# Block-sparse attention into a swish layer: the planner's order replaced by a written one, with new opening casts and paired score steps

## The chip, the cores and the metric

The kernel runs on one core of a Trainium2 chip. Its time is that of one execution in microseconds of device time; before the change three executions took 300.73, 301.71 and 305.26, median 301.71.

## The reference

Attention over four batches of eight heads, 768 positions of 64, in blocks of 32 positions. A query block sees its own block and its two neighbours, the first and the last block, and three blocks drawn per query block (`sampled_blocks`); the first and the last query block see everything. Its output, all heads of a position side by side, goes through a layer of 2048 hidden columns.

```python
scores = scale * np.matmul(q, k.transpose(0, 1, 3, 2))
...
scores = np.where(mask, scores, -1000000000.0)
scores = scores - np.max(scores, axis=-1, keepdims=True)
attn = np.exp(scores)
attn = attn / (np.sum(attn, axis=-1, keepdims=True) + 1e-09)
return np.matmul(attn, v).astype(np.float32)
...
h = x @ w_in
g = h * (1.0 / (1.0 + np.exp(-beta * h)))
return (g @ w_out).astype(np.float32)
```

## The kernel before

**Attention by pairs.** The 22 inner query blocks of a batch are handled in pairs, 44 pairs in all, numbered `n` from 0 to 43. Per pair the program makes these tasks, named by kind and number:

- `kg`: POOL copies six drawn key blocks into the tile `KG` (line 710; the block numbers are loaded to registers first, line 704); `kn`: the neighbour blocks, on POOL or DVE. There are three `KG` buffers.
- `vg`: DMAs on the SP queue that gather value blocks from a table `VT` in memory into `VG` (line 810); for the first four pairs TensorE picks the drawn blocks with one-hot matmuls (`pick`, line 825; `pickv` copies them out).
- `sc`: scores, a first set of matmuls that writes the mask (line 849) and a second that adds the products (line 862), in 64x32 tiles of the array, into two PSUM banks. From pair 33 on, two pairs share one step and take four banks (`TWO = 33`).
- `mx`: maxima on DVE (line 884); `ex`: exponentials on ACT with their sums (line 892), two per bank; `rc` or `hl`: reciprocals on DVE; `nrm`: normalisation of the probabilities `PP`, on POOL (line 915); for pairs below 11 it is folded into the output product (line 953) instead.
- `tp`: transpose on TensorE (line 929) or, from pair 31, by DMA (`tpd`); `ptv`: its copy to `PT` on DVE or ACT (line 330 or 328); `av`: the product with the values (lines 963 and 971); `rs`, `xv`: copies of the result into `xT`, the input of the layer.

The first and last query block of each batch go through `gs`, `gm`, `ge`, `gr`, `gn`, `gt`, `gptv`, `gav`, `gx` (lines 1026 to 1100) with whole rows of 768 scores. K and Q of a batch are loaded, for batch 0 cast on DVE (line 538), transposed on TensorE in half-width tiles (`trK`, `trQ`, line 632) and copied out (`evK`, `evQ`); V is rearranged and written to the table (`vperm`, `permV`, `vtab`).

**The layer.** It works in eight groups `G` of 256 or 512 positions. `h` makes one chunk of 128 hidden columns (line 1155), `tanh` on ACT (line 1161) and `stt` on DVE (line 1166) its activation `g`, `y` a quarter of an output tile (line 1182, four matmuls of 512 columns), `oe` its copy and `od` its DMA. A group's first chunk needs `xT` of the pairs it covers. Weights come by POOL's DMA queue in bulk loads: `win` (line 557, quarters of the hidden columns, two row chunks each), `wout` (line 563), and then K, Q and V of the next batch (line 588). A one-element copy (`touch`, line 543) holds each set back until the value gathers of pair 2 have landed.

**What sets the order.** Every task has an engine or a choice of two, a planned duration, dependencies, a priority, and PSUM banks that it opens or closes. `Plan.run` simulates the engines with these numbers and issues, at each moment, the ready task of the best priority; an `OFFSET` table shifts priorities. Each engine then executes its tasks in the order that comes out, and the bank numbers are those that the plan handed out. Waits between engines are semaphores that follow from the data.

Of the kernel before, what the change touches and what calls it, by code (L numbers as in the profile page):

```python
# [20 lines left out]
BIAS = {("nrm", "DVE"): 2.0, ("gn", "DVE"): 1.5}  # L21


class Task:
    def __init__(self, name, eng, dur, emit, deps=(), prio=0.0, lat=0.0,
                 opens=(), closes=(), moe=False, dma=0.0, slack=0.0, hw=0, bulk=None):
        self.on = {eng: dur} if isinstance(eng, str) else dict(eng)
        self.name, self.eng, self.dur, self.emit = name, None, None, emit
        self.deps = [d for d in deps if d is not None]
# [4 lines left out]
        self.tiling = Plan.TILING.get(self.kind, 0)  # L34
# [3 lines left out]
class Plan:  # L38


    HOP = 0.18
# [3 lines left out]
    MARGIN, DMARGIN = 1.0, 1.0  # L45


    TILING = {"sc": 1, "gs": 1, "av": 2, "gav": 2, "trK": 2, "trQ": 2}
    CHANGE, KEEP = 0.1, 0.0
    YOUNG = {"PE": 0, "DVE": 0, "ACT": 0.0, "POOL": 0.5, "SP": 0.0}  # L50
    YIELD = 20

    OFFSET = {'gt': 5, 'gav': 10, 'trK': 7.6, 'oe': 2.2, 'vg': -0.6, 'vv': -14.0, 'pick': -1.2, 'av0': 0.8, 'ptv0': -3.8, 'xv0': 3.7, 'vg0': 0.9, 'sc1': -2.5, 'kg1': 12.5, 'kn1': -11.1, 'mx1': -15, 'vg1': -5, 'av2': -5, 'kg2': 2.8, 'kn2': 4.2, 'hl2': 5.2, 'rs2': -5, 'kg3': -11.2, 'ex3': 0.3, 'rs3': -0.6, 'kg4': -15, 'rs4': 7.8, 'kn5': 18.1, 'ptv5': 6.3, 'rs5': 39.6, 'av6': -0.3, 'kg6': 2.5, 'kn6': -60, 'ptv6': -2.4, 'mx6': 4.5, 'sc7': 15.7, 'tp7': 21.7, 'av7': 1.3, 'rs7': 1.6, 'sc8': 0.4, 'hl8': -3.7, 'xv8': -17.7, 'av9': -14.9, 'kg9': -6.0, 'kn9': 15, 'mx9': -15, 'ex9': -0.6, 'hl9': 19.8, 'rs9': 15, 'sc10': 21.3, 'tp10': 0.8, 'av10': 15, 'kg10': 2.9, 'kn10': -15, 'mx10': 30, 'vg10': 30, 'sc11': -60, 'av11': 15, 'ex11': 5, 'xv11': -1.7, 'av12': 0.5, 'kn12': -2.5, 'ptv12': 1.2, 'rs12': -0.3, 'xv12': 26.5, 'tp13': -0.2, 'kn13': 4.0, 'rs13': -3.7, 'xv13': -41.1, 'av14': 15, 'kg14': -15, 'kn14': -30, 'rs14': 24.8, 'xv14': 6.6, 'ptv15': 30, 'xv15': -24.7, 'mx0.0': 0.7, 'mx0.1': -9.9, 'mx1.1': -3.1, 'ex1.1': 5.7, 'ex2.0': -2.1, 'ex4.1': -15, 'mx7.1': 56.3, 'gn1': -22.5, 'vperm0.0': -0.6, 'trQ1': 11.7, 'trQ2': 11.1, 'trK3': 2.2, 'trQ3': -0.4, 'castQ': 2.6, 'tabK2': -34.6, 'tabK3': 8.6, 'ttQ2': 19.9, 'ldV3': 0.9, 'pick1': 9.2, 'pickv': 30, 'ldV0.1': 0.1, 'evK0': -6.3, 'evQ0': -1.2, 'tanh0': 5.1, 'stt1': -14.2, 'h3': 0.5, 'y3': -1.4, 'oe3': -8.0, 'y4': 1.4, 'tanh4': 9.0, 'oe4': 1.7, 'h5': 15.9, 'y5': -1.2, 'stt5': 3.2, 'h6': -60, 'y6': 11.9, 'tanh7': 60, 'stt7': -19.4}

    def __init__(self, n_banks, moe_banks):
        self.tasks = []
        self.n_banks, self.moe_banks = n_banks, moe_banks
        self.bank = {}
# [6 lines left out]
    def run(self):  # L65
        tasks = self.tasks
        attention_left = sum(1 for t in tasks if t.opens and not t.moe)
        succ = {}
        need = {}
        for t in tasks:  # L70
            need[t] = len(t.deps)
            for d in t.deps:
                succ.setdefault(d, []).append(t)
        readers = {}
        for t in tasks:
            for b in t.closes:
                readers[b] = readers.get(b, 0) + 1
        ready_at = {t: 0.0 for t in tasks}
        engines = sorted({e for t in tasks for e in t.on})
        free = {e: 0.0 for e in engines}  # L80
        waiting = {e: [] for e in engines}
        ring_at = hw_at = 1.0
        lanes = [0.0] * 8
        issued = 0

        tiling = 0
# [14 lines left out]
        def release(t):  # L101
            for e in t.on:
                waiting[e].append(t)
# [1154 lines left out]
```

## Time and profile before

| | us |
|---|---|
| time, median of three runs (lowest, highest) | 301.71 (300.73, 305.26) |
| span of the profiled execution | 302.9 |
| POOL busy, share of the span | 170.0, 56% |

The profile is that of another execution than the three timed ones, and no time of its own is given beside its span; the span stands between the median and the highest of them. Lines of the trace name the engine, the line of the code, the operation, the tile written and the tiles read. An `x8` behind a row says that eight instructions are merged in it. A time in brackets is the engine's idle time before the row, and what ended it. PE is TensorE's matmuls, PEld its weight loads. In a view of stretches the number after each engine's busy time is its count of instructions, and the last three columns are the granted clock (1.00 is full), the share of time in which the DMA engines were busy, and GB/s.

### The profile page before, as it was taken

How to read it: one execution, taken by the hardware profiler on the slowest of the kernel's cores; microseconds unless marked ns; L12 is line 12 of the kernel's file. 1: busy time of each engine (PE TensorE's matmuls, PEld its weight loads, DVE VectorE, ACT ScalarE, POOL GpSimd, SP SyncE). 2: the span in 40 equal slices, each digit the busy share in tenths (PEclk: the TensorE clock that was granted, in tenths of full speed). 3: DMA queues.
4: the chain of work that ended last, by engine and by line, in shares of the span. 5: the costliest groups of instructions: out<-in, count | busy, mean ns of one | idle time of the engine just before them, and what ended most of it. 6: DMA issues, size and time to landing. Idle time of an engine off the chain costs nothing.

```text
span 302.9 us, 11451 instructions
## 1 busy us (share of the span) xinstructions
PE 279.5 (92%) x4109; PEld 173.8 (57%) x4109; DVE 237.5 (78%) x556; ACT 218.6 (72%) x641; POOL 170.0 (56%) x513
## 2 busy tenths in 40 slices
PE   2599879999998799999999999999999999999993
PEld 1465668758846576665556555545554544555671
DVE  5848987999899998999999739999888834762150
ACT  3357657888789598799889749896787768763360
POOL 5057995034579957899777538677976654000000
PEclk9999957999999999999999999999999999999999
DMA  7999999979978852299933643248465446541102
GB/s 248 365 294 171 205 232 231 228 142 265 213 126 167 181 192 72 84 173 162 237 99 106 202 154 106 67 110 167 120 158 119 126 106 181 137 121 53 53 36 69
DMA packets 57170, 47.55 MB, mean 157 GB/s; under 512 B 19733, under 2 KB 53142, under 8 KB 57114
## 3 DMA queue, kind: packets, MB, share of 16 engines
q1 hardware_dynamic: 44736, 35.48, 41.3%
q0 software_dynamic: 12320, 11.27, 24.7%
q8 instruction: 32, 0.52, 0.7%
q14 instruction: 24, 0.20, 0.2%
q10 hardware_dynamic: 58, 0.07, 0.1%
HBM read 45.23 MB, written 9.44 MB: 180 GB/s over the span
## 4 chain that ended last, share of the span: by engine, by line
PE 49%; DVE 23%; issue 7%; ACT 6%; POOL 6%; DMA 5%; POOLq 2%; SPq 0%; DVEq 0%; ACTq 0%
PE bank L1155 17%; PE bank L1182 14%; DVE ST L884 5%; PE bank L825 4%; DVE g L1166 4%; PE bank L929 3%; POOL KG L710 3%; DMA g<-in_k_dram 3%; DVE SG L1040 3%; POOL PP L915 2%; PE bank L963 2%; PE bank L971 2%; ACT PP L892 2%; PE bank L632 2%; ACT t L1161 2%
## 5 line engine op out<-in xcount | busy, mean ns | idle before, releaser
L1155 PE MATMUL bank<-xT,w_in_sb 128*128 128x256 f16 (+1 forms) x512 | 93.8, 330 | 1.5 <-DVE g L1166 1.5
L892 ACT ACTIVATE PP<-bank,ST 128x256 f16<-128x256 f32 x176 | 81.9, 482 | 15.1 <-DVE ST L884 10.1
L1182 PE MATMUL bank<-w_out_sb,g 128*128 128x512 f16 x384 | 92.0, 379 | 0.0
L1161 ACT ACTIVATE t<-bank,beta_sb 128x512 f16<-128x512 f32 (+1 forms) x128 | 71.0, 595 | 15.7 <-PE bank L1155 10.4
L915 POOL TENSOR_SCALAR PP<-PP,ST 128x256 f16<-128x256 f16 x132 | 63.4, 499 | 30.8 <-DVE ST L909 29.2
L1166 DVE SCALAR_TENSOR_TENSOR g<-t,bank 128x512 f16<-128x512 f16 (+1 forms) x128 | 67.0, 547 | 16.3 <-ACT t L1161 15.8
L1155 PEld LDWEIGHTS <-w_in_sb 128*128 128x128 f16 x512 | 54.4, 115 | 28.1 <-issue 4.1
L710 POOL COPY KG<-KT 128x64 f32 x264 | 52.4, 249 | 25.6 <-PE bank L862 10.5
L884 DVE TENSOR_REDUCE ST<-bank 128x2 f32<-128x512 f32 x88 | 57.6, 680 | 4.2 <-PE bank L862 3.8
L1182 PEld LDWEIGHTS <-g 128*128 128x128 f16 x384 | 35.0, 98 | 37.4 <-issue 3.5
L892 ACT ACTIVATION_READ_ACCUMULATOR PP<-bank,ST 128x1 f32 x176 | 37.4, 212 | 0.0
L1061 POOL TENSOR_SCALAR PG<-PG,SG 128x768 f16<-128x768 f16 x13 | 13.1, 1010 | 24.4 <-ACT PG L1049 15.2
L334 ACT ACTIVATE osb<-bank 128x512 f32<-128x512 f32 (+1 forms) x24 | 14.2, 590 | 16.1 <-PE bank L1182 16.0
L330 DVE COPY PT<-bank 128x1024 f16<-128x1024 f16 x30 | 20.4, 683 | 3.8 <-PE bank L929 3.6
L330 DVE CAST xT<-bank 64x256 f16<-64x256 f32 (+1 forms) x35 | 14.6, 418 | 9.9 <-PE bank L963 6.8
L929 PE MATMUL bank<-identity,PP 128*128 128x128 f16 x248 | 20.4, 225 | 1.2 <-ACT KT L328 0.6
L963 PEld LDWEIGHTS <-VG 128*128 128x128 f16 x448 | 16.1, 98 | 9.2 <-issue 4.3
L1049 ACT ACTIVATE PG<-bank,SG 128x384 f16<-128x384 f32 x32 | 18.3, 589 | 4.2 <-DVE SG L1042 3.6
L929 PEld LDWEIGHTS <-PP 128*128 128x128 f16 x248 | 16.2, 101 | 6.0 <-issue 1.1
L963 PE MATMUL bank<-PT,VG 128*128 128x64 f16 x448 | 17.5, 193 | 2.2 <-DMA PT<-PP 1.5
L330 POOL COPY KG<-KT 128x384 f32<-128x384 f32 (+3 forms) x43 | 16.6, 411 | 1.3 <-PE bank L862 1.3
L328 ACT CAST xT<-bank 64x256 f16<-64x256 f32 (+1 forms) x30 | 11.3, 375 | 8.2 <-PE bank L1089 3.9
(119 smaller groups left out, 317.9 us busy)
## 6 DMA issues: line engine op xcount, KB each, us to landing
VG<-VT SPq DMA_DIRECT2D x220, 32.0 KB, 2.6
VG<-VT SPq DMA_DIRECT2D x32, 192.0 KB, 2.7
out_dram<-osb SPq DMA_DIRECT2D x20, 256.0 KB, 2.1
RV<-in_v_dram POOLq DMA_DIRECT2D x6, 384.0 KB, 6.6
RK<-in_k_dram POOLq DMA_DIRECT2D x6, 384.0 KB, 6.2
VT<-Vn SPq DMA_DIRECT2D x3, 768.0 KB, 3.4
RQ<-in_q_dram POOLq DMA_DIRECT2D x6, 384.0 KB, 6.3
w_in_sb<-in_moe_w_in_dram POOLq DMA_DIRECT2D x8, 256.0 KB, 8.8
```

The lines of the kernel that those rows point to most:

```text
L330: (nc.vector if eng == "DVE" else nc.gpsimd).tensor_copy(out=out, in_=in_)
L710: nc.gpsimd.tensor_copy(out=kg32[:, g, :, (SR + r) * W:(SR + r + 1) * W], in_=kt32[:, :, bass.ds(vals[3 * g + r], W)])
L884: mx[n, u] = add(f"mx{n}.{u}", "DVE", 0.6, lambda n=n, u=u, sb_=sb_: nc.vector.tensor_reduce(out=sb_[:, 0, 2 * u:2 * u + 2], in_=bank(("S" ...
L892: nc.scalar.activation(out=pb[:, u, g, :], in_=bank(("S", n, u))[:, g * 256:(g + 1) * 256], func=AF.Exp, bias=sb_[:, 0, 2 * u + g:2 * u + ...
L915: (nc.vector if eng == "DVE" else nc.gpsimd).tensor_scalar(out=pb[:, u, g, :], in0=pb[:, u, g, :], scalar1=sb_[:, 2, 2 * u + g:2 * u + g + ...
L929: nc.tensor.transpose(out=o[:, s * P:(s + 1) * P], in_=pb[:, u, g, c * P:(c + 1) * P], identity=identity)
L963: nc.tensor.matmul(o[:, (g * NHP + hp) * 2 * BLK:(g * NHP + hp + 1) * 2 * BLK], lhsT=vgb[:, g, c, hp * P:(hp + 1) * P], rhs=pt[:, g, c, :, ...
L1049: nc.scalar.activation(out=pg[:, :].rearrange("x (j p) -> x j p", j=J)[:, :, hf * hw_:(hf + 1) * hw_], in_=bank(("GS", m, hf))[:, 0:S // 2 ...
L1155: nc.tensor.matmul(o[:, 0:TW], lhsT=w_in_v[:, c, f // 4, f % 4, :], rhs=xT[:, c, c0:c0 + TW], start=(c == 0), stop=(c == NHP - 1))
L1161: lambda G=G, f=f, TW=TW, tt=tt: nc.scalar.activation(out=tt[:, 0:TW], in_=bank(("H", G, f))[:, 0:TW], func=AF.Tanh, bias=0.0, scale=beta_ ...
L1166: lambda G=G, f=f, TW=TW, tt=tt, gg=gg: nc.vector.scalar_tensor_tensor(out=gg[:, f, 0:TW], in0=tt[:, 0:TW], scalar=1.0, in1=bank(("H", G, ...
L1182: nc.tensor.matmul(o[:, :], lhsT=gg[:, f, s * P:(s + 1) * P], rhs=w_out_sb[:, f, :], start=(f == 0), stop=(f == N_FFC - 1))
```

## The change

`Plan.run` no longer simulates anything. The tasks are issued in the order of a written list, `ORDER`, of 1723 words: a task's name, for tasks with a choice the engine (A is ACT, D is DVE, G is POOL), and for those that open PSUM banks their numbers. Its beginning, the place of the first hidden chunk, and its end:

```
iota sbl warm ldV0.0 ident ldV0.1 ldK0.0 selc ldK0.1 idx srow mask.0 rowc selb0:0 selb1:1 kl2 vperm0.0 kl0 selw1 kl3
selw0 vtab0.0 kl1 sel16.0 sel16.2 vperm0.1 sel16.4 vtab0.1 sel16.3 castK0.0:A ldQ0.0 sel16.5 sel16.1 ldQ0.1 castK0.1:A
mask.1 trK0.0:0 pick1.0:1 evK0.0:A castK0.2:D castK0.3:A mask.2 trK0.1:2 trK0.2:3 trK0.3:0 pick0.1:4 evK0.2:D evK0.3:A
...
hl5 ldV1.0 h0.0:4 vg6.5 evK1.3:A kn8:D gt1:3 vg5.0 gm3 tanh0.0 ldV1.1 gt0:0 ex7.1 kg10 gm2 ge3 h0.1:2 vg8.4 vg5.2
...
y6.3.1 tanh7.12 stt7.14 stt7.12 y6.3.2 tanh7.15 stt7.15 y6.3.3 stt7.13 y7.0.0:7 y7.0.1 y7.0.2 y7.0.3 y7.1.0:4 oe7.0
```

By engine: ten `ptv` go from DVE to ACT, eleven `nrm` from POOL to DVE, `kn` four more on POOL net, `xv` six more on ACT net. On POOL's queue the bulk loads now stand as `win0.2 win1.2 wout3.1 win1.1 win0.1 win0.0 ldK1.1 win0.3 win1.3 ldK1.0 win1.0 ldV1.0 ldV1.1 ldQ1.0 ldQ1.1`, then the other output weights, the last of them after `ldK2.0`; before, all weights stood ahead of `ldV1.0 ldV1.1 ldK1.0 ldK1.1 ldQ1.0 ldQ1.1`. On SP's queue both `ldQ0` now stand behind `vtab0.0` and `vtab0.1`. The rest of the diff, cut:

```diff
     def run(self):
-        tasks = self.tasks
...
+        by = {t.name: t for t in self.tasks}
+        full = dict(A="ACT", D="DVE", P="PE", G="POOL", S="SP")
         order = []
...
+        for word in ORDER.split():
+            name, _, place = word.partition(":")
+            t = by[name]
+            t.eng = full[place[0]] if place and place[0] in full else next(iter(t.on))
+            t.dur = t.on[t.eng]
+            for b, i in zip(t.opens, place.lstrip("ADPGS")):
+                self.bank[b] = int(i)
+            order.append(t)
...
-    QV = (0, 2)
+    QV = (0, 0)
...
-    TWO, TWOP = 33, 1
+    TWO, TWOP = 11, 1
...
-    VGs = sb("VG", [P, NVG, 2, 2, D_MODEL])
+    VGs = sb("VG", [P, 2, NVG, 2, D_MODEL])[:, :, :, :, :].rearrange("x c n g m -> x n g c m")
...
+    mixed = lambda t: t[:, :, :].rearrange("p h x -> p (h x)").rearrange("p (j m) -> p j m", j=J)
...
-                    f"cast{nm}0.{hp}", "DVE", 0.5,
-                    lambda i=i, dst=dst, hp=hp: nc.vector.tensor_copy(
-                        out=dst[:, 2 * hp:2 * hp + 2, :], in_=stage32(i, hp)),
+                    f"cast{nm}0.{hp}", {"DVE": 0.48, "ACT": 0.74}, None,
+                    lambda eng, i=i, dst=dst, hp=hp: copy_on(
+                        eng, mixed(dst)[:, :, hp * P:(hp + 1) * P].rearrange("p j (u d) -> p u j d", u=2),
+                        stage32(i, hp).rearrange("p u (j d) -> p u j d", j=J)),
...
-    for fq in range(4):
-        fs = slice(fq * FQ * P, (fq + 1) * FQ * P)
-        for c in range(0, 4, 2):
+    for f in range(2):
+        fs = slice(f * D_FF // 2, (f + 1) * D_FF // 2)
+        for c in range(NHP):
...
-            th = add(f"h{G}.{f}", "PE", 4 * (TW / 2400.0 + 0.003), emit_h, deps=xdeps + t_win[f // 4 * 2:f // 4 * 2 + 2],
+            th = add(f"h{G}.{f}", "PE", 4 * (TW / 2400.0 + 0.003), emit_h, deps=xdeps + t_win[f // 8 * NHP:f // 8 * NHP + NHP],
...
+                    if b == 0:
+                        for j in range(J):
+                            nc.tensor.transpose(out=o[:, j * P:(j + 1) * P],
+                                                in_=mixed(s16)[:, j, hp * P:(hp + 1) * P], identity=identity)
+                        return
...
+        kl = add(f"kl{n}", "POOL", 0.45, emit_kl, deps=[t_idx, t_rc], prio=-1) if n < NKL else None
...
-            evs.append(add(f"xv{n}.{u}", {"DVE": 0.42, "ACT": 0.38}, None, emit_xv, deps=[av[n]], prio=pr - 0.5,
+            evs.append(add(f"xv{n}.{u}", {"DVE": 0.42, "ACT": 0.38}, None, emit_xv, deps=[av[n]] + evs, prio=pr - 0.5,
...
-        gi = (G + (sizes[0] < 8)) % NG if G or sizes[0] >= 8 else 0
-        gc = TW if G == 1 and sizes[0] < 8 else 0
+        gi, gc = ((0, 0), (0, 256), (1, 0), (0, 0), (1, 0), (0, 0), (1, 0), (0, 0))[G]
...
-                te.emit, te.on = lambda ob=ob, G=G, s=s: scale_on(
-                    "ACT", ob[:, 0:256], bank(("Y", G, s))[:, 0:256], 0.5), {"ACT": 0.35}
-                tf = add(f"of{G}.{s}", "DVE", 0.35, lambda ob=ob, G=G, s=s: scale_on(
-                    "DVE", ob[:, 256:512], bank(("Y", G, s))[:, 256:512], 0.5), deps=list(te.deps), prio=te.prio,
-                    closes=(("Y", G, s),))
```

In words: the opening casts of K and Q may run on ACT and write the two heads of a head pair side by side, so that batch 0's transposes are six whole 128x128 ones per head pair (12 half-width ones before); the input weights load as two halves of the hidden columns, one row chunk per DMA, and a hidden chunk needs the four loads of its half; the value tile holds its two halves apart in memory; the block numbers of the first four gathers are loaded to registers ahead (`kl`); two pairs share a score step from pair 11 on where both lie in one batch; the Q loads no longer wait for V; the second half of an `xv` waits for the first; the layer's second group writes `g` beside the first group's instead of into the other buffer; and the last output tile leaves PSUM in one copy on ACT. Planned durations are set anew throughout; with a written order they set nothing.

More of the change, by code (lines that the diff above doesn't have):

```diff
@@ L80, in run @@
[L80 to L86, printed above, removed]
-        off = {t: t.prio + self.OFFSET.get(t.name, self.OFFSET.get(t.name.split(".")[0], self.OFFSET.get(t.kind, 0.0)))
-               for t in tasks}
-        def rank(t, e):
-            young = now - ready_at[t] < self.YOUNG[e] - 1e-9
-            return off[t] + (self.KEEP if e == "PE" and t.tiling != tiling else 0.0) + (self.YIELD if young else 0.0)
```

378 lines of the change are left out of this document (179 added, 199 removed).

## Prediction

> **What bounds the kernel now.** I read the busy times first, then stretches of the span, then what the matmul engine waits for, and last the order of time at the places that the change touches.
>
> ```profile
> span 302.9 us, 11451 instructions
> PE 279.5 (92%) x4109; PEld 173.8 (57%) x4109; DVE 237.5 (78%) x556; ACT 218.6 (72%) x641; POOL 170.0 (56%) x513
> ```
> ```profile
> 24.00:45.00 21.00, 18.04 (x441) 12.97 (x420) 19.39 (x48) 14.91 (x57) 19.65 (x69) 0.85 1.11 201
> 45.00:92.00 47.00, 47.00 (x831) 33.52 (x830) 43.03 (x117) 38.61 (x119) 21.24 (x54) 0.96 1.02 201
> 92.00:110.00 18.00, 14.37 (x282) 10.81 (x283) 17.60 (x38) 13.93 (x44) 15.00 (x40) 1.00 0.81 193
> 110.00:270.00 160.00, 156.97 (x2239) 90.14 (x2234) 134.57 (x289) 130.43 (x384) 105.91 (x311) 1.00 0.55 133
> ```
>
> Columns of the second view: stretch, length, busy time of PE, PEld, DVE, ACT, POOL, granted clock, DMA share, GB/s. PE has work in 47.00 of 47 us and 156.97 of 160: over two thirds of the span PE is the bound, and the 25 us that DVE and the 30 us that ACT have free in the long stretch are cover. Two holes remain: 24 to 45 us (DVE 19.39 and POOL 19.65 of 21 are the tight ones, and the clock is down), and 92 to 110 us, where 3.6 us of PE are empty. What PE waits for, over the whole span (total, times, longest):
>
> ```profile
> PE bank L849 <- DVE ST L884: 2.2, 1, 2.2
> PE bank L963 <- DMA PT<-PP: 1.5, 3, 0.7
> PE bank L1155 <- DVE g L1166: 1.5, 1, 1.5
> PE bank L963 <- ACT PP L892: 0.2, 1, 0.2
> ```
>
> So a new order can win only three things: less PE work, fewer of these waits, an earlier first score. I price each.
>
> **Fewer visits to the scores.** In PE's instruction order the scores of pairs 12 to 32 lose ten steps, and separate visits fall from 35 to 26. The trace has both kinds: one pair per visit early, two per visit from pair 33.
>
> ```profile
> 60.62 1.89 PE L1182 MATMUL bank<-w_out_sb,g 128*128 128x512 f16 x8
> 62.44 0.28 PE L849 MATMUL bank<-maskr,ones 64*32 64x192 f16 x8
> ...
> 62.87 1.04 PE L1182 MATMUL bank<-w_out_sb,g 128*128 128x512 f16 x4
> ```
> ```profile
> 237.25 1.89 PE L1182 MATMUL bank<-w_out_sb,g 128*128 128x512 f16 x8
> 239.07 0.36 PE L849 MATMUL bank<-maskr,ones 64*32 64x192 f16 x16
> ...
> 239.80 1.05 PE L1155 MATMUL bank<-xT,w_in_sb 128*128 128x512 f16 x4
> ```
> ```profile
> 274.04 1.73 PE bank L1182 x8
> ```
>
> Eight output matmuls take 1.73 us in a run; here the scores start 1.82 after them, so entering costs 0.09. A one-pair visit then lasts 0.43, a two-pair visit 0.73. Two visits cost 2 x 0.52 = 1.04, the double one 0.82: 0.22 each, times 9 is -2.0 us, on the bound itself. Bounds: 0 (the freed time is filled by a wait) and -3.1 (if leaving costs as much as a whole pair, 0.34).
>
> **Waits in mid-run.** I laid out PE's order with durations from the trace (0.216 us per 512-column matmul as above, smaller ones by columns) and counted the PE work between a pair's scores and its output product: in the old order 3.0 to 4.8 us for pairs 3 to 5 and about 11 in the median of pairs 11 to 40; in the new one 8 to 17 and about 21. The latency that must fit in between (two maxima, four exponentials, normalisation, transpose, copy) is mostly under 11, so waits on it shrink. From 110 to 270 us PE is empty for 3.0 us, half of it the wait for transposes above; I take -2.0 (bounds 0 and -3.0).
>
> **The hole at 92 to 110.** Its root is on POOL's queue, in order:
>
> ```profile
> 62.46 0.91 POOL L1061 TENSOR_SCALAR PG<-PG,SG 128x768 f16<-128x768 f16 x1 [13.04 <-ACT PG L1049]
> 63.33 0.80 POOL L588 DMA_DIRECT2D RK<-in_k_dram  x1
> ...
> 73.44 0.79 POOL L588 DMA_DIRECT2D RQ<-in_q_dram  x1
> 75.17 1.12 POOL L710 COPY KG<-KT 128x64 f32 x6 [0.94 <-DVE KT L330]
> ```
>
> POOL stands 13 us behind a global-row normalisation, and the second batch's K and Q loads stand behind it, so that batch's keys are gathered only at 75 us. The new list puts one K half seventh among the bulk loads and all Q loads ahead of the late output weights, with the global scores before pair 6 instead of after the first products. That frees the batch-1 chain by some 10 us; what is late next is DVE, at 17.60 of 18. I take -3.0 of the 3.6 (bounds 0 and -6, if the small stalls at tiling changes go as well). Queued behind POOL's global normalisation stays one quarter of the input weights, which the ninth hidden chunk needs; its cover is seven chunks and the pairs between.
>
> **The opening.**
>
> ```profile
> 9.70 1.03 DVE L538 CAST RK<-g 128x768 f16<-128x768 f32 x2 [0.80 <-DMA g<-in_k_dram]
> ...
> 12.57 1.49 PE L632 MATMUL bank<-identity,RK 128*64 128x128 f16 x24 [0.77 <-DVE RK L538]
> ...
> 13.47 1.50 ACT L328 COPY KT<-bank 128x768 f16<-128x768 f16 x2 [0.75 <-PE bank L632]
> ...
> 13.99 1.94 PE L825 MATMUL bank<-Vn,xT 128*96 128x512 f16 x4
> ...
> 15.03 2.65 POOL L710 COPY KG<-KT 128x64 f32 x12 [10.32 <-ACT KT L328]
> ...
> 23.43 0.33 PE L849 MATMUL bank<-maskr,ones 64*32 64x320 f16 x8
> ...
> 24.01 0.30 POOL L543 COPY w_in_sb<-VG 1x1 f16<-1x1 f16 x2 [4.12 <-DMA VG<-VT]
> ```
>
> K still lands at 9.7. Three of its four casts go to ACT; no row has that form, the nearest are DVE's 0.52 and ACT's 0.75 for 128x768, and I take 0.75. On PE a pick of six 0.43 us matmuls now stands before the second transpose, and a transpose with heads side by side has half the matmuls over twice the columns: six full 128-column ones for twelve half-width ones that run two at a time (24 in 1.3 us), so no gain. That gives 9.7 + 0.75 + 0.65 + 2.6 + 3 x 0.65 = 15.7 and two ACT copies of 0.75, so K is ready at about 17.2, not 15.0. Then POOL runs three gathers of 1.3 and one neighbour copy of 1.1: first scores at 22.2 against 23.43. Q is issued on SP behind both V-table writes and lands no earlier than before; ACT copies it out by 21, under that. The gate of the weights opens at about 22.2 instead of 24.0. DVE then has, up to the fourth pair's xT, 16 maxima where it had 13 and two global maxima more, against two pick copies, two transposed copies and a neighbour copy fewer: about the same sum, so the first hidden chunk gains only this 1.2. I take -1.2; bounds -3 and +2 (POOL gathers slowed beside the casts). The split of the input weights by rows makes the first chunk wait for four loads, not two; they are ordered early and the DVE chain above covers them.
>
> **The clock.**
>
> ```profile
> 40.00:44.00 4.00, 4.00 (x79) 3.32 (x66) 3.26 (x11) 2.19 (x10) 3.37 (x14) 0.50 1.17 235
> ...
> 48.00:52.00 4.00, 4.00 (x80) 3.56 (x74) 3.06 (x9) 3.32 (x10) 1.42 (x2) 0.89 1.09 229
> ```
>
> After the 2.2 us wait PE runs at half clock until about 49: up to 4 us of PE work lost, while DVE is the tight engine for the first half. The new order still leaves PE short of work there; I take -1.5, bounds 0 and -4. [...]
>
> **Engines off the path.**
>
> ```profile
> L915 POOL TENSOR_SCALAR PP<-PP,ST 128x256 f16<-128x256 f16 x132 | 63.4, 499 | 30.8 <-DVE ST L909 29.2
> L330 DVE COPY PT<-bank 128x1024 f16<-128x1024 f16 x30 | 20.4, 683 | 3.8 <-PE bank L929 3.6
> ```
> ```profile
> 89.56 0.60 DVE L330 COPY Vn<-RV 128x1536 f16<-128x1536 f16 x1
> ...
> 103.08 2.67 DVE L330 COPY Vn<-RV 128x1536 f16<-128x1536 f16 x1
> ```
>
> Ten transposed-probability copies go from DVE to ACT (-6.8 on DVE), eleven normalisations from POOL to DVE. No DVE row has them; four operations each, between 0.2 (a third of the 0.60 copy, six times the size) and POOL's own 0.5, so 9 to 22 us of DVE time, hidden by the 25 free. I cost both at 0; without the cover they would cost +2. [...] The last evacuation, two half-width copies, becomes one of full width on ACT:
>
> ```profile
> 298.33 0.38 ACT L334 ACTIVATE osb<-bank 128x256 f32<-128x256 f32 x1 [2.86 <-PE bank L1182]
> 298.74 0.42 DVE L336 TENSOR_SCALAR osb<-bank 128x256 f32<-128x256 f32 x1 [6.39 <-ACT osb L334]
> ```
>
> The DVE half ends at 299.16; a full one on ACT, at most 0.76, ends by 299.09: nothing.
>
> **Sum.** -2.0 - 2.0 - 3.0 - 1.2 - 1.5 = -9.7, so 293.2 against the profiled span of 302.9. The runs before have a median of 301.7, 0.4% under that span; so I predict 292.
>
> **Rivals.** *Full clock and a closed hole.* If PE's waits before 45 us stay short, the clock term is -4 and the hole gives -6: 292 - 5.5 = 286.5. For it: the longer distances. Against: DVE and POOL are full there. *Nothing much.* PE is full in 47.00 of 47; if the holes only move, the visits alone are left: 299.5. For it: attention before 45 us is set by DVE work, which grows up to the first hidden chunk. *Banks run short: slower.* A double visit holds four of eight banks until eight exponentials are done, in order on ACT ahead of the hidden chunks' tanh.
>
> ```profile
> L892 ACT ACTIVATE PP<-bank,ST 128x256 f16<-128x256 f32 x176 | 81.9, 482 | 15.1 <-DVE ST L884 10.1
> ```
>
> The second pair's four are 1.9 us that a hidden chunk's bank may stand longer; over ten new doubles up to 19 us. From 1 us each it eats the gain; at 1.7 each the time is 309. Against: after the doubles of the trace PE goes straight on, and waits for exponentials are 0.2 in all.
>
> **Chances and range.** Forecast 0.46 (288 to 296), full clock 0.17, nothing much 0.22, banks 0.15. What a measurement here can tell from no change is about 2%, so under 295.7 and over 307.7. Faster 0.46 x 0.92 + 0.17, with a little of the third, 0.61; slower two thirds of the last, 0.11; the rest 0.28. The range 284 to 304 leaves out about 2 in 10, mostly of the slow case.
>
> **What would show it.** 26 separate visits to the scores; first scores at 22; no POOL wait of 13 us and the second batch's keys well before 75 us; PE over 17 of 18 us between 92 and 110; half clock shorter than 10 us. Wrong it is if PE waits for a bank behind exponentials, for the K load of batch 1 or for the last input weights, or if PE is idle in 50 to 90, where it is full now.

## The result, and the profile after

The changed kernel took 305.49 us (median of 12 runs, 303.68 to 312.69) against 301.94 (12 runs, 300.32 to 305.74) before: ratio 1.011, 95% interval 1.008 to 1.014. It is slower by about 1%; 292.0 was predicted. Executions marked as slow (one of 312.69 us, at a mean granted clock of 0.958) are left out of the ratios, of the experiments' times and of the reading here, which takes a second profile of this kernel, from beside the first experiment. Its page and its stretches:

```profile
span 304.8 us, 11270 instructions
PE 275.5 (90%) x4061; PEld 175.3 (58%) x4061; DVE 225.8 (74%) x562; ACT 229.3 (75%) x662; POOL 157.4 (52%) x485
```
```profile
24.00:45.00 21.00, 15.07 (x323) 9.89 (x323) 16.86 (x50) 17.43 (x67) 13.71 (x50) 0.83 1.00 187
45.00:92.00 47.00, 41.08 (x909) 31.16 (x906) 40.02 (x116) 42.38 (x130) 33.54 (x91) 0.93 1.03 203
92.00:110.00 18.00, 17.42 (x472) 14.95 (x476) 17.73 (x41) 17.20 (x54) 15.34 (x46) 1.00 0.56 123
110.00:270.00 160.00, 156.30 (x1984) 91.64 (x1967) 126.16 (x294) 125.41 (x366) 85.44 (x255) 1.00 0.60 145
```

The hole at 92 to 110 is closed (17.42 of 18, before 14.37). But PE, which was full in 47.00 of 47 between 45 and 92, now has work in 41.08, and in 15.07 instead of 18.04 of the 21 us ahead. Half clock is longer too: from the clock column 2 x 0.17 x 21 + 2 x 0.07 x 47 = 13.7 us, before 10.1.

Busy time hides how much was done, since a matmul at half clock counts long (eight transposes of 128x128 in the kernel before: 0.62 us at 32.5 us, 1.03 at 42.6, at half clock). So I counted each matmul by its columns at full rate, by one rule in all kernels, and added up what PE had done by a given time (for e11 without 44 matmuls that do nothing). A small tile counts for less here than the time it takes (32 matmuls of 32 columns are 0.43 us at the rate of the wide ones, 0.216 us for 512 columns, and last 0.66 in the kernel before), so a stretch's figure also depends on which work falls into it:

```
us of PE work done by             24 us   45 us   92 us  110 us  270 us   span
before                             10.1    23.3    64.6    75.7   222.5  302.9
changed                            12.1    21.8    54.8    69.8   220.6  304.8
old order, new code (e2)           11.2    22.9    64.8    74.8   220.5  304.8
old order, the change's loads (e7) 11.0    23.1    55.0    69.7   211.7  313.8
cured old order (e11)              11.6    25.3    66.1    79.0   227.1  298.2
```

e2, e7 and e11 are explained below. Against before, the changed kernel is 2.0 us ahead at 24, 9.8 behind at 92, 5.9 behind at 110 and 1.9 behind at 270. So it wins 2.0 in the opening, loses 11.8 between 24 and 92, wins 3.9 in the hole and 4.0 behind it. The first scores, and POOL's waits for a global normalisation (the longest 7.0 us, no longer 13, and that one at 260 us):

```profile
21.81 0.28 PE L833 MATMUL bank<-maskr,ones 64*32 64x192 f16 x8
```
```profile
POOL PG L1047 <- DVE SG L1044: 16.3, 3, 7.0
```

What PE waits for from 24 to 92 (total, times, longest):

```profile
PE bank L1140 <- issue: 2.6, 1, 2.6
PE bank L833 <- ACT PP L877: 1.7, 3, 1.2
PE bank L609 <- DMA RK<-in_k_dram: 1.3, 1, 1.3
PE bank L846 <- POOL KG L694: 1.2, 1, 1.2
PE bank L833 <- ACT PG L1035: 0.9, 1, 0.9
PE bank L1140 <- ACT PP L877: 0.8, 1, 0.8
PE bank L914 <- ACT PP L877: 0.7, 1, 0.7
PE bank L1140 <- ACT PG L1035: 0.5, 1, 0.5
```

No single wait carries it. The first is a stop for code, explained below. The others are links of the attention chain (exponentials on ACT, gathers on POOL, the K load), which PE now meets with nothing to put between. The waits of L833 and L1140 for ACT are for a bank that exponentials still read: 3.9 us in all, against 0.8 before, and all of them end by 57 us, ahead of the first of the new double steps at 80. What stood between before were the first group's hidden chunks and output products. From 45 to 92 us PE spends 32.1 us on these two kinds before (L1155 and L1182) and 20.2 after (L1140 and L1167). The loads that those need, on POOL's queue and in PE's order, before and after:

```profile
37.34 0.53 POOL L563 DMA_DIRECT2D w_out_sb<-in_moe_w_out_dram  x1
...
46.11 1.02 POOL L563 DMA_DIRECT2D w_out_sb<-in_moe_w_out_dram  x2
47.12 1.55 POOL L588 DMA_DIRECT2D RV<-in_v_dram  x2
```
```profile
57.06 1.24 PE L1182 MATMUL bank<-w_out_sb,g 128*128 128x512 f16 x5
```
```profile
35.65 0.76 POOL L560 DMA_DIRECT2D RK<-in_k_dram  x1
...
47.70 1.56 POOL L560 DMA_DIRECT2D RV<-in_v_dram  x2
...
55.01 0.58 POOL L535 DMA_DIRECT2D w_out_sb<-in_moe_w_out_dram  x1
...
66.54 0.51 POOL L535 DMA_DIRECT2D w_out_sb<-in_moe_w_out_dram  x1
```
```profile
81.47 1.03 PE L1167 MATMUL bank<-w_out_sb,g 128*128 128x512 f16 x4
```

The last output weight is issued at 66.5 instead of 46.6, and the first output product runs at 81.5 instead of 57.1. The two loads that this first product needs landed at 45.0 and 46.6 before; after, they land at 72.0 and 73.4. Until then the weights hold it back; for the last 8 us the list's own order of PE does. That is a reading of two traces; the experiments test it.

### The profile page after: what moved, and what is told of

It is laid out like the page before. It is cut to its first block, busy times and chain, and to the rows that moved or that the text cites. A ratio compares the mean times of both kernels' runs of the same rounds, so it can differ in the third digit from the quotient of the medians.

```text
span 310.9 us, 11270 instructions
## 1 busy us (share of the span) xinstructions
PE 280.6 (90%) x4061; PEld 178.0 (57%) x4061; DVE 226.4 (73%) x562; ACT 229.7 (74%) x662; POOL 157.4 (51%) x485
## 3 DMA queue, kind: packets, MB, share of 16 engines
q0 software_dynamic: 11296, 11.27, 23.4%
## 4 chain that ended last, share of the span: by engine, by line
PE 61%; DVE 14%; issue 3%; ACT 2%; DMA 1%; SPq 0%; DVEq 0%; ACTq 0%
PE bank L1167 24%; PE bank L1140 23%; PE bank L948 5%; DVE ST L869 3%; DVE g L1151 3%; PE bank L846 2%; PE bank L914 2%; PE bank L833 1%; DVE PT L300 1%; DVE SG L1026 1%; PE bank L609 1%; DVE PTG L1063 1%; ACT PP L877 1%; PE bank L1055 1%; PE bank L1075 1%
## 5 line engine op out<-in xcount | busy, mean ns | idle before, releaser
L1140 PE MATMUL bank<-xT,w_in_sb 128*128 128x512 f16 (+1 forms) x512 | 98.9, 336 | 3.2 <-DVE SG L1028 1.7
L1151 DVE SCALAR_TENSOR_TENSOR g<-t,bank 128x256 f16<-128x256 f16 (+1 forms) x128 | 67.6, 548 | 37.1 <-ACT t L1146 36.7
L1146 ACT ACTIVATE t<-bank,beta_sb 128x256 f16<-128x256 f32 (+1 forms) x128 | 72.0, 593 | 28.6 <-PE bank L1140 20.2
L1167 PE MATMUL bank<-w_out_sb,g 128*128 128x512 f16 x384 | 92.3, 381 | 0.0
L1140 PEld LDWEIGHTS <-w_in_sb 128*128 128x128 f16 x512 | 55.0, 115 | 33.6 <-issue 9.2
L1167 PEld LDWEIGHTS <-g 128*128 128x128 f16 x384 | 36.0, 98 | 38.4 <-issue 3.1
L900 POOL TENSOR_SCALAR PP<-PP,ST 128x256 f16<-128x256 f16 x88 | 43.0, 506 | 26.0 <-DVE ST L894 12.0
L877 ACT ACTIVATION_READ_ACCUMULATOR PP<-bank,ST 128x1 f32 x176 | 38.4, 218 | 0.0
L300 POOL COPY KG<-KT 128x384 f32<-128x384 f32 (+3 forms) x55 | 20.4, 404 | 20.4 <-PE bank L846 19.6
L304 ACT ACTIVATE osb<-bank 128x512 f32<-128x512 f32 x24 | 14.4, 605 | 17.1 <-PE bank L1167 15.3
L300 DVE CAST xT<-bank 64x256 f16<-64x256 f32 (+1 forms) x29 | 12.1, 418 | 10.8 <-PE bank L948 10.0
L914 PE MATMUL bank<-identity,PP 128*128 128x128 f16 x248 | 19.1, 222 | 0.7 <-ACT PP L877 0.7
L846 PE MATMUL bank<-KG,QT 64*32 64x256 f16 x704 | 16.1, 278 | 0.8 <-POOL KG L694 0.7
L298 ACT CAST xT<-bank 64x256 f16<-64x256 f32 (+1 forms) x36 | 13.5, 375 | 4.2 <-DVE xT L300 2.3
```

The source lines that it names most:

```text
L300: (nc.vector if eng == "DVE" else nc.gpsimd).tensor_copy(out=out, in_=in_)
L846: nc.tensor.matmul(bk[u][hp * BLK:(hp + 1) * BLK, g * 256:(g + 1) * 256], lhsT=QT[b % 2][u * D:(u + 1) * D, hp, (i0 + g) * BLK:(i0 + g + 1 ...
L877: nc.scalar.activation(out=pb[:, u, g, :], in_=bank(("S", n, u))[:, g * 256:(g + 1) * 256], func=AF.Exp, bias=sb_[:, 0, 2 * u + g:2 * u + ...
L900: (nc.vector if eng == "DVE" else nc.gpsimd).tensor_scalar(out=pb[:, u, g, :], in0=pb[:, u, g, :], scalar1=sb_[:, 2, 2 * u + g:2 * u + g + ...
L914: nc.tensor.transpose(out=o[:, s * P:(s + 1) * P], in_=pb[:, u, g, c * P:(c + 1) * P], identity=identity)
L1140: nc.tensor.matmul(o[:, 0:TW], lhsT=w_in_v[:, c, f // 4, f % 4, :], rhs=xT[:, c, c0:c0 + TW], start=(c == 0), stop=(c == NHP - 1))
```

## The experiments

Theory A: the list starves PE between 24 and 92 us. Theory B: double score steps hold four banks too long. Theory C: the edits of the code cost, not the order. Two more came up on the way: F, PE stops for its own code; D, value gathers share a full DMA with the weights. "Old order" below is the planner's order of the kernel before, written out as words with its banks and engines and run through the new code.

**e1_after_again**, the changed kernel as it is.

> The changed kernel once more, to have a profile beside the timed runs. All theories: 304 to 307 us, ratio about 1.01. Theory A (the new list starves the matmul engine early): its idle time between 24 and 110 us is 5 us or more above the old kernel's, which shows 3.0 us of empty PE in 24 to 45, none in 45 to 92 and 3.6 in 92 to 110; after 110 us it is no larger than the old one's. Theory B (double score steps hold four banks): the extra idle time stands after 110 us, behind exponentials. Theory C (the code edits, not the order): it stands in the opening, before 24 us.

304.62 us, ratio 1.0096 (1.0054 to 1.0138). This is the profile read above.

**e2_old_order**, all edits but the order.

```diff
-ORDER = """ iota sbl warm ldV0.0 ident ...
+ORDER = """ sbl warm ident ldV0.0 ldV0.1 ...
-    NKL = 4
+    NKL = 0
-    TWO, TWOP = 11, 1
+    TWO, TWOP = 33, 1
```

> The new code with the old kernel's order, engines and banks written into the list, single score steps up to pair 32 and no early register loads. What stays of the change: the casts' layout and whole transposes, the value tile's layout, the weights by halves, the g buffers, one last copy. A and B: within 1% of the old kernel, 300 to 304 us. C: 304 to 307 us, as slow as the changed kernel.

303.39 and 306.65 us, no interval; 307.86, the figure that later expectations use, is the median of four executions, these two among them. Two times 3.3 us apart settle little by themselves. e5 below, the same order with nine runs and a median of 304.89, says that the new code is as slow with the old order as with the new one, as theory C has it and against theory A alone. Since the order is the same, each matmul can be set against itself. The start of the same PE instruction, less its start in the kernel before (negative is earlier; by its time before; e10 to e14 follow below):

```
at           24     36     45     57    102    111    201    291 us
e2        -1.18   2.19   0.20  -0.34  -0.21   1.57   1.35   2.08
e10       -1.40  -1.06  -3.70   3.21   3.21   1.31   1.25   0.86
e11       -1.50  -0.91  -3.40  -1.84  -1.82  -3.73  -3.89  -4.49
e12       -1.36   0.00  -1.57  -1.93  -1.93  -0.64  -0.75  -0.29
e14       -0.90   1.98   0.48  -0.11   0.43  -1.47  -2.33  -1.96
```

The opening wins 1.2 us, the figure forecast for the change, but by another way: the casts stay on DVE here, and it is Q's second set of transposes that starts at 20.19 instead of 21.21. The gain is gone by 36. The timeline of e2 shows where:

```profile
32.60 0.38 PE L847 MATMUL bank<-KG,QT 64*32 64x256 f16 x9
36.07 0.30 PE L847 MATMUL bank<-KG,QT 64*32 64x256 f16 x7 [3.09 <-issue]
```

PE stops inside one score step, between two matmuls with the same inputs, at an instruction without a semaphore. The trace also has transfers on queues named "instruction". The row of the changed kernel's page (packets, MB, share):

```profile
q8 instruction: 32, 0.52, 0.7%
```

That is 16 KB each, and 2 x 4061 matmuls and weight loads make 254 PE instructions per transfer. Every stop of this kind falls on the same series of instruction numbers, 706 plus multiples of 256 (20 stops of over 0.9 us in the 16 traces, each exactly on it; PE's semaphore records are counted too), and lasts until 2.2 to 2.5 us after the start of such a transfer. Times are the profile's; the recorded texts count from 0.26 us later:

```
kernel    stop at   lasts   PE instruction   transfer starts
before      37.11    2.43              962             37.32
e1          68.97    2.91             1986             69.46
e2          32.71    3.36              706             33.90
e14         33.17    2.92              706             33.89
```

So I read these stops as PE out of code; no view names the cause. In quiet stretches the transfer mostly starts within a microsecond or so of PE passing the edge ahead (DMA share 0.55 from 110 to 270 us in the kernel before); between 25 and 70 us, with the DMA engines always busy (1.02 to 1.11 there), it is mostly 2 to 4 us late, at most 4.7, and a dense burst of small matmuls runs its 256 instructions sooner than that (2.4 us in e2). The kernel before has such a stop too, which the prediction took for a wait for DVE's maxima:

```profile
36.12 1.28 DVE L884 TENSOR_REDUCE ST<-bank 128x2 f32<-128x512 f32 x2
```
```profile
39.54 0.36 PE L849 MATMUL bank<-maskr,ones 64*32 64x192 f16 x7 [2.17 <-DVE ST L884]
```

These maxima end at 37.40, and PE goes on 2.1 us later; the next ones, until 39.01, are of pair 5, on banks that this step doesn't write. Data held PE for the first half of that: an exponential reads the bank of its next matmul until 37.8, and the neighbour keys that the products need are copied by 38.4. So about 1.1 of the 2.2 us are the stop's own, an estimate from these rows.

**e3_old_first** and **e4_new_first**: hybrids, the one with the old order up to the hidden chunk `h1.0` and the new one from there, the other with the new order up to the scores of pair 11 and the old one from there; banks dealt anew.

```diff
-ORDER = """ (the change's list)
+ORDER = """ (e3: old list up to h1.0, then the change's words that are left)
+ORDER = """ (e4: the change's list up to sc11, then the old words that are left; TWO = 33)
```

> The new code; the list is the old order up to the end of the first group's output (old order's first 69 us), and from there what is left in the new order, double score steps from pair 12 on, banks handed out anew in list order. A: the loss is gone and the later gain stays, 295 to 301 us. B: still slow, 303 to 308 us. C: 304 us or more.

> The mirror image: the new order up to just before the scores of pair 11, and from there what is left in the old order, single score steps to pair 32, banks handed out anew. A: slow, 303 to 308 us. B: the loss is gone, 298 to 303 us. C: 304 us or more.

317.1 us, ratio 1.046 (1.038 to 1.054), and 313.3, ratio 1.035 (1.029 to 1.041): both worse than either parent. By 92 us e4 has done 56.4 us of PE work, as little as the changed kernel, which puts that loss into the new beginning; but e3 loses at its seam (12.0 us of work from 65 to 92, before 24.5), so neither verdict on the whole counts for much.

**e5_old_shifted**, e2 with the edges of the code blocks moved.

```diff
             nc.tensor.matmul(o, lhsT=ones[0:1, :], ..., start=False, stop=True)
+            for _ in range(44 * f):
+                nc.tensor.matmul(banks[7][0:4, 0:4], lhsT=identity[0:4, 0:4], rhs=identity[0:4, 0:4],
+                                 start=True, stop=True)
```

> The new code with the old order (as e2_old_order), and 44 tiny matmuls (88 TensorE instructions with their weight loads) added in the opening, into a bank that nothing reads, while TensorE waits anyway. Theory F (TensorE's own code): in e2_old_order TensorE stops 3.4 us at 32.45 inside one score step, at an instruction that has no wait, and the transfer that carries the next 256 of its instructions starts only at 33.64, 3.6 us after the block before was begun; 256 instructions took 2.4 us there. 88 more instructions in front move the edges of the blocks so that the tightest 256 take 4.4 us: the stop shrinks to about 1.4 us and moves to an earlier instruction, the half clock behind it may shorten, and the time comes to 303 to 306 against the 307.9 of e2_old_order. Rival (TensorE waits there for data, or the code edits cost elsewhere): the stop stays at the same matmul with the same length and the time stays near 307.9 or above.

304.89 us, ratio 1.0115 (1.0081 to 1.0149). The stop inside that score step is gone; two short ones appear at instructions 962 (1.0 us) and 1218 (1.7 us), on the same series. (The trace is of its longest execution, 308.15 us; e10's shows the same waits for gathers.) But PE, 4.1 us ahead of the kernel before at 48 us, then stands 5.1 us for value gathers and is behind again. Theory F holds; what is late next is the DMA.

**e6_new_loads_late**, in the changed list.

```diff
-av5:3 vg9.1 ldK2.0 tanh0.10 ... ge4 ldV2.0 stt0.11 ... ex12.0 ldK2.1 mx13.1
+av5:3 vg9.1 tanh0.10 ... ge4 stt0.11 ... ex12.0 ldK2.0 ldV2.0 ldK2.1 mx13.1
```

> The changed kernel with two words of its list moved: the first key load and the first value load of batch 2 (384 KB each, issued at 61.1 and 66.8 us) go behind the output weights, to the place of the second key load (82.7 us). Theory F: the block of code that TensorE needs at 68.7 us was asked for at 65.1 and started at 69.2, behind these loads; with less traffic it comes sooner, the stop of 2.9 us at 68.7 falls below 1.5 us, and with it the 3.4 us of half clock behind it: 301 to 304 us. Theory A (the list starves TensorE between 24 and 92 us, whatever the code does): less than 1 us, 304.5 to 306.

306.06 us, ratio 1.0157 (1.0082 to 1.0232). The stop is 2.58 us long instead of 2.91, but with the loads in place it is 2.0 in the profile beside the result and 1.7 in e9: those two loads do not hold the code up. Theory F's forecast for this run failed. Its time says less, since PE stands another 3.1 us at 97.2 behind DVE, which takes 5.0 us for two copies of value rows. Here and in e1:

```profile
94.43 5.01 DVE L300 COPY VG<-VG 32x2048 f16<-32x2048 f16 x2
```
```profile
95.01 1.58 DVE L300 COPY VG<-VG 32x2048 f16<-32x2048 f16 x2
```

**e7_old_order_new_loads**, e2 with batch 1's loads ahead of most output weights, as the change has them.

```diff
+ldK1.0 ldK1.1
 wout0.0 ... wout0.1
+ldQ1.0 ldQ1.1
 ... wout1.0 ... wout1.1
+ldV1.0 ldV1.1
 ... wout2.0 ... wout3.1
-... ldV1.0 ldV1.1 ldK1.0 ldK1.1 ldQ1.0 ldQ1.1
```

> The new code with the old order (as e2_old_order), but with the loads of batch 1 ahead of most output weights, as the change has them: both key loads ahead of the first output weight, both query loads ahead of the third, both value loads ahead of the fifth. Theory A: this load order is what keeps TensorE without output matmuls in 45 to 92 us. 2.3 MB more ahead of the weights, at the pace of the eight output loads themselves (2 MB in 9.3 us), puts them up to 10 us later; TensorE stands before its first output matmuls, 5 to 9 us more idle in 45 to 92, of which 2 to 4 come back in 92 to 110 because the keys of batch 1 are there: 310 to 314 us. Rival (the weights have slack, the loss lies elsewhere): within 2 us of e2_old_order, 306 to 310, or faster by the hole in 92 to 110 (304 to 306).

317.28 us (2 runs), ratio 1.053 (1.043 to 1.063). Stretches of it, and PE at its first output products:

```profile
45.00:92.00 47.00, 39.28 (x643) 27.98 (x636) 34.78 (x100) 29.99 (x87) 13.27 (x32) 0.89 0.78 168
92.00:110.00 18.00, 17.54 (x347) 10.74 (x346) 16.55 (x41) 15.18 (x52) 13.71 (x39) 1.00 0.86 156
```
```profile
59.07 1.04 PE L1168 MATMUL bank<-w_out_sb,g 128*128 128x512 f16 x4 [1.09 <-DMA w_out_sb<-in_moe_w_out_dram]
...
66.92 1.89 PE L1168 MATMUL bank<-w_out_sb,g 128*128 128x512 f16 x4 [4.98 <-DMA w_out_sb<-in_moe_w_out_dram]
```

The signature of the change on the old order: 39.28 of 47 us, the hole behind it closed (17.54 of 18), and by 92 us 55.0 us of work done against 64.8. Theory A in this form is shown for the old order, and the price, some 12 us over e2, is larger than expected. In e7 PE waits for the weights. The change's list was written around their coming late, so PE waits there for other things and has less to run between.

**e8_blend**: every word at a place between its old and its new one.

> The new code with a list in between: every task at its old place in time up to 80 us, going over to its place in the changed list by 200 us, banks dealt anew, one pair per score step throughout. Theory A: TensorE is no further behind the kernel before at 92 us than e2_old_order is, and idles as little behind 110 us as in the changed kernel (7 to 9 us in 110 to 270 against 13): 299 to 303 us. Theory B (the double score steps or the way banks are dealt decide): without double steps the part behind 110 us is no better than before, and banks dealt anew cost as in the two hybrids: 308 us and more.

375.8 us, ratio 1.249 (1.241 to 1.258). Every engine waits for every other, most of all POOL for DVE: places in two lists can't be averaged. The run speaks for neither theory.

**e9_single_scores**, the changed list with ten doubles split where they stand.

```diff
-sc12:2546
+sc12:25 sc13:46
```

> The changed kernel with its ten double score steps below pair 33 split into two steps that stand side by side in the list, on the same banks (sc12 on 2546 becomes sc12 on 25 and sc13 on 46). Theory B (a step that holds four banks and makes two pairs wait for each other costs behind 110 us): the maxima of the first pair can start some 0.4 us earlier per step, 2 us or more are won, 301 to 303.5. Theory A (the loss is made before 92 us): ten visits more at 0.28 us of switching at most, less the earlier maxima: 304 to 307, no gain outside the interval.

304.7 us, ratio 1.0089 (1.0049 to 1.0129), the same as the change. Theory B falls. The banks open at the same places as in the change, so the run tests only the tie between two pairs; against the prediction's rival of the short banks speaks e1's trace, where PE waits for exponentials 0.2 us in all behind 110 us.

**e10_perm_later**, e5 with one DVE copy later. In e2 it stands here, and PE behind it:

```profile
103.00 2.92 DVE L301 COPY Vn<-RV 128x1536 f16<-128x1536 f16 x1
```
```profile
106.31 0.60 PE L1141 MATMUL bank<-xT,w_in_sb 128*128 128x256 f16 x4 [1.86 <-DVE g L1152]
```

```diff
-stt2.3 ... permV2.1 nrm14 ... mx16.0 tanh2.9
+stt2.3 ... nrm14 ... mx16.0 permV2.1 tanh2.9
```

> As e5_old_shifted, and one VectorE copy of the old order (the value rows of batch 2 put in order, 128x1536, 2.9 us at 103 us in e2_old_order, while TensorE waits 1.9 us for VectorE's product and ScalarE 2.7 us) moved behind the maxima of pair 16, some 12 VectorE instructions later. If that copy makes the wait, it goes, and with it the half clock behind it (108 us, 3.4 us long): 1.5 to 3.5 us under e5_old_shifted, 300.5 to 303.5. If the copy only takes the place of another wait, the wait moves to the transposes of batch 2 or to the next product: within 1 us of e5_old_shifted.

302.77 us, ratio 1.0014 (0.9975 to 1.0054), 1% under e5: the copy made the wait. Moved, it takes 0.62 us, at 111.7, though POOL's normalisations run beside it there too. The kernel before has the same slow copy (2.67 us at 103.08) and a wait of 1.5 us behind it, so this move mends nothing that the change did; it would be open to that kernel too. The waits for gathers are still there:

```profile
50.66 0.24 PE L960 MATMUL bank<-PT,g 128*64 128x32 f16 x2 [3.15 <-DMA g<-VT]
53.28 0.99 PE L960 MATMUL bank<-PT,g 128*64 128x32 f16 x30 [2.38 <-DMA g<-VT]
```

**e11_perm_weights_later**, e10 with the first seven output weights later on POOL's queue (the first some 2.5 us later).

```diff
-mx4.0 wout0.0 ... hl3 wout0.1 ... tp4 wout1.0 ... xv3.0 wout1.1 ...
+rs3 wout0.0 ... kg10 wout0.1 ... av5 wout1.0 ... vv8 wout1.1 ...
```

> As e10_perm_later, and the output weights' loads 1 to 7 moved back by 2 to 4 us each on the POOL queue (the first from 37 to about 41 us); the first output matmul needs them at 56. Theory D (the value gathers of the pairs at 47 to 53 us, on the SP queue, share a full DMA with the weights, so whatever TensorE wins before 47 is lost waiting for them): the gathers land 2 us or more earlier, the 5.1 us that e5_old_shifted waits for them fall under 3, and what the opening and the missing stop won (4.1 us at 47) is kept in part: 297 to 301 us, under the kernel before. Rival: the gathers are held by the SP queue's own order or the weights come late: the same as e10_perm_later within 1 us, or up to 3 us slower with TensorE waiting for output weights.

300.57 us, ratio 0.9954 (0.9911 to 0.9996): faster than the changed kernel, and by 0.5% than the one before. Its stretches:

```profile
24.00:45.00 21.00, 17.39 (x462) 12.65 (x461) 20.39 (x53) 16.13 (x62) 19.04 (x71) 1.00 1.04 199
45.00:92.00 47.00, 45.14 (x795) 31.93 (x794) 42.47 (x113) 37.77 (x118) 22.55 (x54) 1.00 1.08 212
92.00:110.00 18.00, 16.45 (x388) 13.01 (x386) 17.40 (x42) 16.36 (x50) 15.91 (x47) 1.00 0.70 155
```

The wait for gathers falls from 5.5 to 1.8 us, SP has issued the last of them by 47.0 us instead of 49.1, full clock is granted throughout, and the opening's gain stays to the end (the row of e11 above). Against the kernel before the interval just leaves out no change; against e10, ten runs each on one chip, e11 is 2.6 us faster in the mean (95%: 1.1 to 4.0). The two traces overstate it: e10's is of an execution of 305.43 us, near its longest, e11's of 300.08.

**e12_old_input_loads**, e5 with the input weights loaded as before.

```diff
-    for f in range(2):
-        for c in range(NHP): ... out=w_in_sb[:, c, fs], in_=w_in_r[:, c, fs]
+    for fq in range(4):
+        for c in range(0, 4, 2): ... out=w_in_sb[:, c:c + 2, fs], in_=w_in_r[:, c:c + 2, fs]
```

> As e5_old_shifted, with the input weights loaded as in the kernel before (eight loads of 1 KB rows, a quarter of the columns of two row blocks each, two for the first hidden chunk instead of four). Theory D: in the new code these loads moved 0.17 MB more than before by 45 us and the gathers 0.15 MB less; with the old loads the gathers land sooner, the 5.1 us of waiting at 47 to 53 shrink by 2 us or more: 301 to 303. Rival (the form of the loads does not matter, only that TensorE comes early): within 1 us of e5_old_shifted, 304 to 306.

304.16 us, ratio 1.0052 (1.0012 to 1.0092). In its profile PE does not wait for gathers at all between 24 and 110; in time it lies under e5, but the intervals overlap slightly. PE comes later here than in e10 (-1.57 at 45, against -3.70), but the product that got its gathers at 53.3 in e10 has them by 49.6. That fits theory D without proving that the form of the loads alone is the cause.

**e13_all_three** and **e14_unshifted**: the edits of e10, e11 and e12 together, and the same without the 44 small matmuls.

> The new code with the old order, and everything that won so far together: the 44 small matmuls in front, the input weights loaded as in the kernel before, the copy of value rows behind the maxima of pair 16, the output weights' loads 2 to 4 us later. If the three prices are separate (theory D: each is a wait of its own on the way of TensorE), 1 to 3 us under e11_perm_weights_later at best and 297.5 to 300 us. If they overlap (gathers that come in time either way), the same as e11_perm_weights_later, 299.5 to 301.5.

> As e13_all_three without the 44 small matmuls, so that the edges of TensorE's code blocks lie as in e2_old_order. Theory F: the stop inside the score step at 32 us comes back (2 to 3.4 us, the half clock behind it), 1 to 4 us slower than e13_all_three. Rival (with the loads as before the code blocks come in time anyway, as the kernel e12_old_input_loads had no such stop): no stop over 1 us, the same within 1 us.

300.83 us, ratio 0.9966 (0.9934 to 0.9998), and 303.37, ratio 1.0100 (1.0036 to 1.0164). The two differ by nothing but 44 matmuls whose result no one reads, and the kernel that runs them is faster by 2.5 us in the median, 3.3 in the mean (95%: 1.7 to 4.9). Without them PE stops again at instruction 706:

```profile
36.09 0.30 PE L847 MATMUL bank<-KG,QT 64*32 64x256 f16 x7 [2.65 <-issue]
```

The stop for code is a cost of its own. e13 is no better than e11, so the old form of the input loads and the later output weights seem to cure the same wait.

## Why the prediction was wrong

**Most gains came.** *Opening*, -1.2: the first scores run at 21.8 us (22.2 forecast, 23.4 before), K being ready at 16.6 (17.2 forecast), and 2.0 us more work is done by 24. *The hole*, -3.0: measured -3.9. *Visits*, -2.0: they fall from 35 to 26, as counted. *Mid-run waits*, -2.0: they did not shrink, PE is empty for 3.7 us from 110 to 270 (3.0 before). PE does 4.0 us more counted work in that stretch, together what the two terms forecast, but that is luck: hidden chunks and output products take 129.4 us of it, 116.8 before, because they were pushed there from 45 to 92. What the visits brought by themselves stays open. *The end*, 0: +0.5 between 270 us and the last matmul, and 0.6 less behind it. *Engines off the path*, 0: the normalisations that went to DVE take 11.2 us there (9 to 22 forecast), with no price seen. Of the two copies of 128x1536 that this part shows, the long one (2.67 us) ran beside POOL's normalisations of 103.28 to 105.11 us; but in e10 such a copy takes 0.62 us beside four of them, so they alone do not make it long.

**The step that failed** stands in the part on the hole: "The new list puts one K half seventh among the bulk loads and all Q loads ahead of the late output weights", "That frees the batch-1 chain by some 10 us; what is late next is DVE". It booked a load moved forward as a gain and put no price on the loads moved back behind it. What was late next were the output weights, and with them the filling that kept PE full in 47.00 of 47: 11.8 us of counted work lost from 24 to 92, more than the 9.7 of the whole sum. The prediction named it as a sign of error ("if PE is idle in 50 to 90, where it is full now"), as it did the waits for a bank behind exponentials (3.9 us) and for batch 1's K load (1.3), but gave that case no price among its rivals. e7 shows the mechanism on the old order. For the changed list it is argued in part: the weights that its first output product needs are there 8 us before it runs, so the list's order of PE has a share, and so may the global scores that it places early. That the list would be cured by weights first was not tried, since its order of PE would have to be written anew.

**The clock**, -1.5: the sign was wrong, half clock is some 3.5 us longer. The 2.2 us wait on which that term rested was, for its second half, not a wait for maxima but a stop for code, by the reading above, and the new order did not remove such stops but moved them: in the changed kernel one fell at 69.0 us (2.6 us idle). Single waits do not tell where the clock drops: two of that kernel's three drops from 24 to 92 us stand ahead of 45 us, where no wait of PE is over 1.3, and e11 keeps full clock with stops of 2.0. In these traces the granted clock changes on a grid of 3.41 us (half clock in the kernel before lasts 10.24, three steps, from 38.67 to 48.91 us), and what goes with a drop is the share of one grid window in which PE is empty, whatever it waits for. Of the 40 drops ahead of 290 us in the 16 profiles, 36 follow a window that is empty for 48% or more; of the 1184 windows behind which full clock went on, 5 are, at most 55%. In the changed kernel the three windows begin at 24.3, 41.4 and 68.7 us and are 58, 63 and 76% empty; only the third holds a stop for code.

**The code edits**, priced at nothing beyond the opening: on the old order they leave the span 1.9 us longer (e2). The opening's gain meets a stop for code at 32, then, where that is gone, gathers at 50, and around the slow DVE copy at 103 another 1.8 us more than before are lost: the wait there is 0.4 us longer (1.86 against 1.47), and half clock follows it in e2 and not in the kernel before (granted clock from 92 to 110 us 0.95 and 1.00). With three small moves the same code beats the kernel before by 0.5% (e11), but at least one of these, the copy's, was open to that kernel too and was not tried on it. So neither the edits nor the order alone made the result: with the old order and with the new one the new code runs about 305 us, and the written order, with its losses and gains, is worth about nothing on it.

**Rivals.** *Full clock*: its condition held, no wait from 24 to 45 us is over 1.3, and half clock came twice all the same. *Banks running short*: the double steps cost nothing (e9), and behind 110 us waits for exponentials are 0.2 us in all; the bank waits that did come stand ahead of the doubles. Its 309 was nearest to the measured time, for a mechanism that is not there.

## What to carry to other kernels

With the DMA engines at a share of 1.00 to 1.11 from 24 to 92 us, before and after, the loads moved forward here put the last output weight back from 46.6 to 66.5 us. Where transfers are as dense, find out which work was covering the bound engine, and what its loads are, before booking a gain. When two kernels share an order, subtract the start of each instruction from itself; the curve is flat except where something was won or lost, and shows in one look what an average over the span hides. The opening's 1.2 us in e2 were gone by 36 us, at the stop for code, and e5's 4.1 us by 53, at the gathers: a gain ahead of a stretch limited by something else lasted here until that limit, so cure waits in the order in which the work meets them.

## What the hardware showed that was not expected

- The page lists 32 transfers of 16 KB named "instruction" (e1, 0.7% of the time of the same 16 DMA engines that carry the data), one for every 254 PE instructions, and PE stopped at fixed instruction numbers, 256 apart: 20 stops of 1.0 to 3.4 us in the 16 traces, shown as "issue" or put down to a semaphore long set. In e2 it was amid dense small matmuls (256 instructions in 2.4 us) and busy DMA engines (share 1.06 from 24 to 45 us). 44 idle matmuls in front were worth about 3 us (2.5 in the median, e13 against e14).
- Half clock came in stretches of 3.41 us and multiples, mostly 3.41, 6.83 and 10.24, 36 of 40 times after a window of 3.41 us in which PE was empty for 48% or more. e11, with stops of 1.0, 2.0 and 2.0 us between 36 and 50, kept full clock until its end: its emptiest window there is 51%, the others 33% at most.
- One DVE copy held PE up for 1.86 us (e2, at 106.31). The copy of 128x1536 took 2.92 us in e2 and 0.62 in e10, both beside POOL's normalisations; of six copies of 32x2048 in e6 one took 4.4, the others 0.7. What makes the long ones is not shown.
